# Interleaving the two halves of x and of the output weights in one tile, with a different run length in each block of a chunked-attention and gated-FFN kernel

## The chip, the cores and the metric

The kernel runs on one core of a Trainium2 chip. The metric is the device time of one execution in microseconds (us), lower is better. Each number of the trace comes from one execution recorded by the hardware profiler.

## The reference

Attention within chunks of 64 positions, then a gated feed-forward layer on the attention's output. Cut to what is computed:

```python
# q, k, v: (8, 8, 576, 64) float32; chunk = 64
scores = np.matmul(q_c, k_c.transpose(0, 1, 2, 4, 3)) / np.sqrt(64)
attn = np.exp(scores - scores.max(-1, keepdims=True))
attn = attn / (attn.sum(-1, keepdims=True) + 1e-09)
x = np.matmul(attn, v_c)          # laid out as 4608 tokens x 512
g, val = x @ w_gate, x @ w_val    # 512 x 1536 each
out = (g * sigmoid(g) * val) @ w_out      # 1536 x 512
```

## The kernel before

The 4608 tokens are cut into nine blocks (b = 0 to 8) of N = 512 tokens. In a block the attention writes x transposed: features on the 128 partitions in NK = 4 pieces k, the block's 512 tokens along the free axis. The feed-forward layer then goes through NF = 12 pieces f of 128 hidden features. For each f TensorE makes

- the gate (`gate`, g = 0) and the value (`value`, g = 1), each one PSUM bank of 128 x 512, and
- the projection (`project`), which multiplies the hidden piece by 128 rows of the output weights and adds into four PSUM banks `ps_o`, one for each 128 tokens, over all twelve f.

All these products are made in `float32r`, a 32-bit type of reduced precision, so each factor is split into an upper half (the rounded value) and a lower half (the remainder), and a product is the sum of three matmuls: lower times upper, upper times lower, upper times upper. The helper `split` (L62) makes the halves: ScalarE casts to the upper half (L64), VectorE subtracts it from the source to get the lower (L65).

A matmul has a stationary operand of 128 x 128, loaded by LDWEIGHTS, and a moving operand of 128 x 512 that is streamed past it. In the gate and the value (`some`, L419, matmul on L423) the stationary operand is a piece of the gate or value weights and the moving operand is x: `xh` or `xl`, 512 neighbouring words in each partition. In the projection (L466 to L469) the stationary operand is a 128-token piece of the hidden features (`hh` or `hl`) and the moving operand is the output weights of this f: `woh` or `wol`, again 512 neighbouring words.

So a block has 12 x 2 x 12 = 288 matmuls on L423 and 12 x 4 x 3 = 144 on L467 to L469, 432 in all, every one with 512 columns.

The halves of x are made once for a block: in blocks 0, 1 and 2 by `upper` (L541, ScalarE) and `lower` (L545, VectorE) from PSUM, in the later blocks by `ready` and `split` from the tile `s_sb`. They lie in the pool `xs`, tiles `xh0`, `xl0`, `xh1`, `xl1`, two buffers each. The halves of the output weights are made anew for each f of each block by `out_weights` (L425) from weights that stay in SBUF; they lie in the pool `wp`, tiles `woh` and `wol`, two buffers each. Two of these buffers also serve at the start as a place for attention values of block 1 (L526).

The order of the work on TensorE, ScalarE and VectorE is the order of the code (`manual_schedule`). Blocks 0 and 1 are interleaved while the weights are still being loaded and unpacked; the projections of block 1 are put off and follow together with the attention of block 2. Blocks 2 to 8 are written by `block` (L795): for each f the gate, the value, the output weights, and then, by `lag`, the projection of the f before; the attention of block b + 1 is spread between the f's of block b.

## Time and profile before

| quantity | value |
|---|---|
| time, median of two runs | 952.54 us (952.51 and 952.57) |
| the profiled execution's own time | 953.59 us |
| its span, first to last instruction | 951.8 us |
| TensorE's granted clock over the span | 1.0 |
| busy: PE, PEld, DVE, ACT | 944.4, 779.2, 479.5, 337.2 us |

PE is TensorE's matmul stream, PEld its loading of stationary operands, DVE is VectorE, ACT is ScalarE, POOL is GpSimd and SP the engine that issues most DMAs. The row of a group of instructions names the line of the code, the engine, the operation, the tile written and the tiles read, the shape, the number of instructions and after the bar their busy time and the mean duration of one in ns. Matmuls overlap each other in the pipeline, so the duration of one (390 ns for 512 columns) is longer than the distance from one to the next; what the stream takes is read from start times. A row of a table by stretches of time has the length of the stretch, then the busy time and the number of instructions of each engine.

### The profile page before, as it was taken

How to read it: one execution, taken by the hardware profiler on the slowest of the kernel's cores; microseconds unless marked ns; L12 is line 12 of the kernel's file. 1: busy time of each engine (PE TensorE's matmuls, PEld its weight loads, DVE VectorE, ACT ScalarE, POOL GpSimd, SP SyncE). 2: the span in 40 equal slices, each digit the busy share in tenths (PEclk: the TensorE clock that was granted, in tenths of full speed). 3: DMA queues.
4: the chain of work that ended last, by engine and by line, in shares of the span. 5: the costliest groups of instructions: out<-in, count | busy, mean ns of one | idle time of the engine just before them, and what ended most of it. 6: DMA issues, size and time to landing. Idle time of an engine off the chain costs nothing.

```text
span 951.8 us, 14613 instructions
## 1 busy us (share of the span) xinstructions
PE 944.4 (99%) x6299; PEld 779.2 (82%) x6299; DVE 479.5 (50%) x783; ACT 337.2 (35%) x540; POOL 6.6 (1%) x14
## 2 busy tenths in 40 slices
PE   8999999999999999999999999999999999999998
PEld 6788888888888888888888888888888888888886
DVE  6966666573465236632574347533663256432221
ACT  4745444265242333233323233233423342332222
POOL 1100000000000000000000000000000000000000
PEclk9999999999999999999999999999999999999999
DMA  9514322443300230021102030023002210000001
GB/s 360 216 68 155 155 108 103 156 166 112 89 1 1 90 87 3 1 90 63 27 0 88 2 90 1 3 86 90 1 1 89 67 23 1 1 15 30 1 1 44
DMA packets 43792, 63.85 MB, mean 67 GB/s; under 512 B 27472, under 2 KB 27472, under 8 KB 42320
## 3 DMA queue, kind: packets, MB, share of 16 engines
q1 hardware_dynamic: 42000, 59.78, 18.3%
q10 hardware_dynamic: 1728, 3.15, 0.9%
q8 instruction: 49, 0.80, 0.3%
q14 instruction: 15, 0.12, 0.0%
HBM read 50.33 MB, written 12.58 MB: 66 GB/s over the span
## 4 chain that ended last, share of the span: by engine, by line
PE 98%; DMA 1%; DVE 0%; SPq 0%; issue 0%; ACT 0%
PE ps_gv L423 62%; PE ps_o L467 10%; PE ps_o L468 10%; PE ps_o L469 10%; PE ps_a L226 2%; PE ps_a L306 1%; DMA qk_t<-in_qk 1%; PE ps_a L412 1%; PE ps_a L398 1%; PE ps_a L364 0%; DVE s_sb L392 0%; PE unread L60 0%; DVE top L358 0%; SPq L200 0%; ACT o_sb L474 0%
## 5 line engine op out<-in xcount | busy, mean ns | idle before, releaser
L423 PE MATMUL ps_gv<-xh,w 128*128 128x512 f32 x1728 | 531.1, 390 | 0.0
L423 PEld LDWEIGHTS ps_gv<-xh,w 128*128 128x128 f32 x1728 | 324.0, 188 | 67.2 <-issue 0.2
L423 PE MATMUL ps_gv<-xl,w 128*128 128x512 f32 x864 | 335.8, 391 | 0.0
L448 DVE SCALAR_TENSOR_TENSOR h<-ps_gv,h 128x512 f32<-128x512 f32 x108 | 74.6, 691 | 364.1 <-PE ps_gv L423 357.4
L423 PEld LDWEIGHTS ps_gv<-xl,w 128*128 128x128 f32 x864 | 162.2, 188 | 34.8 <-issue 0.4
L441 ACT ACTIVATE h<-ps_gv 128x512 f32<-128x512 f32 x108 | 64.6, 599 | 312.4 <-PE ps_gv L423 312.3
L467 PE MATMUL ps_o<-woh,hl 128*128 128x512 f32 x432 | 168.4, 390 | 0.0
L468 PE MATMUL ps_o<-wol,hh 128*128 128x512 f32 x432 | 168.1, 389 | 0.0
L469 PE MATMUL ps_o<-woh,hh 128*128 128x512 f32 x432 | 168.1, 389 | 0.0
L64 ACT CAST hh<-h 128x512 fp32r<-128x512 f32 x96 | 59.7, 621 | 183.3 <-DVE h L448 183.3
L467 PEld LDWEIGHTS ps_o<-woh,hl 128*128 128x128 f32 x432 | 81.1, 188 | 16.9
L469 PEld LDWEIGHTS ps_o<-woh,hh 128*128 128x128 f32 x432 | 81.1, 188 | 16.8
L468 PEld LDWEIGHTS ps_o<-wol,hh 128*128 128x128 f32 x432 | 81.1, 188 | 16.7
L293 DVE STREAM_TRANSPOSE turned<-s_sb 32x256 f32<-32x256 f32 x192 | 83.6, 436 | 2.7
L65 DVE TENSOR_TENSOR wol<-wo,woh 128x512 fp32r<-128x512 f32 x108 | 73.8, 684 | 13.1 <-ACT woh L64 13.0
L65 DVE TENSOR_TENSOR hl<-h,hh 128x512 fp32r<-128x512 f32 x96 | 66.4, 692 | 18.2 <-ACT hh L64 11.1
L64 ACT CAST woh<-wo 128x512 fp32r<-128x512 f32 x108 | 66.2, 613 | 15.6 <-DVE wo L102 15.6
L226 PEld LDWEIGHTS ps_a<-qk_t 64*64 64x64 f32 x1152 | 18.5, 137 | 5.0 <-issue 3.0
L226 PE MATMUL ps_a<-qk_t 64*64 64x64 f32 x1152 | 20.3, 223 | 0.5 <-DMA qk_t<-in_qk 0.4
L99 DVE TENSOR_TENSOR t<-t 128x1024 bf16<-128x1024 bf16 (+1 forms) x13 | 8.5, 651 | 22.7 <-ACT t L91 22.5
L474 ACT ACTIVATE o_sb<-ps_o 128x512 f32<-128x512 f32 x36 | 18.8, 599 | 2.2 <-PE ps_o L469 2.0
L136 ACT CAST w<-t 128x1024 fp32r<-128x1024 f32 x11 | 11.6, 1056 | 16.7 <-DVE t L102 16.7
(63 smaller groups left out, 411.5 us busy)
## 6 DMA issues: line engine op xcount, KB each, us to landing
raw<-in_wgv SPq DMA_DIRECT2D x11, 1024.0 KB, 7.0
qk_t<-in_qk SPq DMA_DIRECT2D x10, 1024.0 KB, 7.7
out<-o_sb SPq DMA_DIRECT2D x36, 256.0 KB, 2.3
qk_t<-in_qk SPq DMA_DIRECT2D x16, 512.0 KB, 4.0
raw<-in_wo SPq DMA_DIRECT2D x6, 1024.0 KB, 4.9
v_t<-in_v SPq DMA_DIRECT2D x28, 128.0 KB, 2.8
h<-h ACTq DMA_DIRECT2D x12, 256.0 KB, 2.0
h_in<-h SPq DMA_DIRECT2D x6, 512.0 KB, 3.6
```

The lines of the kernel that those rows point to most:

```text
L64: nc.scalar.copy(out=hi, in_=src)
L65: (engine or nc.vector).tensor_tensor(out=lo, in0=src, in1=hi.bitcast(F32), op=ALU.subtract)
L136: nc.scalar.copy(out=self.w[:, 0], in_=self.t)
L226: nc.tensor.matmul(ps[h][j * C:(j + 1) * C, i, u // 2, :], part[:, us:us + C], part[:, M * P + us:M * P + us + C], start=not more or i + u ...
L293: nc.vector.transpose(out=self.turned[to:to + 32, p:p + 2, j, :, 32 * (i % 2):32 * (i % 2) + 32], in_=src[32 * i:32 * i + 32, :, o // 2, 3 ...
L423: nc.tensor.matmul(ps, w, x, start=first and (k, i) == which[0], stop=last and (k, i) == which[-1])
L441: nc.scalar.activation(h, pg, AF.Silu, scale=2.0 ** -8)
L448: nc.vector.scalar_tensor_tensor(out=h, in0=pv, scalar=2.0 ** -8, in1=h, op0=ALU.mult, op1=ALU.mult)
L467: nc.tensor.matmul(o, hl[:, ts], woh, start=f == 0, stop=False)
L468: nc.tensor.matmul(o, hh[:, ts], wol, start=False, stop=False)
L469: nc.tensor.matmul(o, hh[:, ts], woh, start=False, stop=f == NF - 1)
L474: nc.scalar.activation(o_sb, o, AF.Copy, scale=2.0 ** -8)
```

## The change

The upper and the lower half no longer have tiles of their own. They share a tile twice as wide and lie in it in alternating runs of g columns: g words of the upper half, g words of the lower, and so on. The run length depends on the block: `RUN` gives 512 (N), 512, 1, 2, 16, 32, 64, 128 and 256 for blocks 0 to 8. With 512 the two halves lie one behind the other, as two tiles would. In the blocks with a shorter run the 512 words of a half are spread over 1024 words: with g = 1 every second word is taken, with g = 2 two words of every four, with g = 256 two stretches of 256 words.

```diff
+RUN = (N, N, 1, 2, 16, 32, 64, 128, 256)
 class Attn:
         def places(self):
-            self.x = [(xs.tile([P, 2, N], F32R, name=f"xh{c}"), xs.tile([P, 2, N], F32R, name=f"xl{c}"))
-                      for c in range(NP // 2)]
+            self.x = []
+            for c in range(NP // 2):
+                x = xs.tile([P, 2 * 2 * N], F32R, name=f"x{c}").rearrange(
+                    "p (i n o g) -> p i n o g", i=2, o=2, g=RUN[self.b])
+                self.x.append((x[:, :, :, 0], x[:, :, :, 1]))
...
+    def runs(a, g):
+        return a.rearrange("p (n g) -> p n g", g=g)
...
     def some(ps, a, f, g, which, first=True, last=True):
...
-            nc.tensor.matmul(ps, w, x, start=first and (k, i) == which[0], stop=last and (k, i) == which[-1])
+            nc.tensor.matmul(runs(ps, RUN[a.b]), w, x, start=first and (k, i) == which[0], stop=last and (k, i) == which[-1])
 
-    def out_weights(f, engine=None):
-        woh = wp.tile([P, DM], F32R, name="woh")
-        wol = wp.tile([P, DM], F32R, name="wol")
-        split(wo_raw[f], woh, wol, engine)
+    def out_weights(f, b, engine=None):
+        w = wp.tile([P, 2 * DM], F32R, name="wo").rearrange("p (n o g) -> p n o g", o=2, g=RUN[b])
+        woh, wol = w[:, :, 0], w[:, :, 1]
+        split(runs(wo_raw[f], RUN[b]), woh, wol, engine)
         return woh, wol
...
-            ts, o = slice(t * P, (t + 1) * P), a.o[t]
+            ts, o = slice(t * P, (t + 1) * P), runs(a.o[t], RUN[a.b])
...
-            pool, tag = (ld, "v_t") if a is a0 else (wp, ("woh", "wol")[c])
+            pool, tag = (ld, "v_t") if a is a0 else (wp, "wo")
```

`upper`, `lower` and `ready` view their source through `runs` in the same way, so that source and target have the same shape. In the built program the PSUM output of every matmul is still 512 neighbouring words, the stationary operands are as before, and the number and the order of the instructions on PE, ACT, DVE, POOL and SP are the same as before. What differs is the pattern in which three kinds of operand are laid out in SBUF: the moving operand of the 432 matmuls of each of the blocks 2 to 8, the targets of the ScalarE casts and of the VectorE subtractions that make the halves, and the subtraction's second input.

On VectorE, in block 3 (the ninth and the tenth f), the rows before are, with `wol` and `xl` the lower halves written and `xh` and `woh` the upper halves read:

```order
L448 SCALAR_TENSOR_TENSOR h<-ps_gv,h 128x512
L65 TENSOR_TENSOR wol<-wo_1357,woh 128x512
L65 TENSOR_TENSOR hl<-h,hh 128x512
L448 SCALAR_TENSOR_TENSOR h<-ps_gv,h 128x512
L65 TENSOR_TENSOR wol<-wo_1457,woh 128x512
L65 TENSOR_TENSOR hl<-h,hh 128x512
L65 TENSOR_TENSOR xl_3829<-s_sb,xh_3828 128x512 x2
```

And the same place after the change, where `x` and `wo` hold both halves:

```order
L457 SCALAR_TENSOR_TENSOR h<-ps_gv,h 128x512
L67 TENSOR_TENSOR wo<-wo_1346,wo 128x256x2
L67 TENSOR_TENSOR hl<-h,hh 128x512
L457 SCALAR_TENSOR_TENSOR h<-ps_gv,h 128x512
L67 TENSOR_TENSOR wo<-wo_1445,wo 128x256x2
L67 TENSOR_TENSOR hl<-h,hh 128x512
L67 TENSOR_TENSOR x_3774<-s_sb,x_3774 128x32x16 x2
```

No instruction has moved. The output weights of block 3 are written as 256 runs of 2 words; the x written here is already that of block 4, in 32 runs of 16.

More of the change, by code (lines that the diff above doesn't have):

```diff
@@ L322, in ready @@
             for p in range(p, p + n):
-                split(self.s[:, p].rearrange("p c h k -> p (c h k)"), *(x[:, p % 2] for x in self.x[p // 2]))
+                split(runs(self.s[:, p].rearrange("p c h k -> p (c h k)"), RUN[self.b]),
+                      *(x[:, p % 2] for x in self.x[p // 2]))
     class First(Attn):
@@ L473, in project @@
                 o_sb = pool.tile([P, DM], F32, name="o_sb", tag=tag)
-                nc.scalar.activation(o_sb, o, AF.Copy, scale=2.0 ** -8)
+                nc.scalar.activation(o_sb, a.o[t], AF.Copy, scale=2.0 ** -8)
                 r = a.b * N + t * P
@@ L540, in upper @@
     def upper(a, px, p):
-        nc.scalar.copy(out=x_of(a, p)[0], in_=px[p % 2])
+        nc.scalar.copy(out=x_of(a, p)[0], in_=runs(px[p % 2].rearrange("p u k -> p (u k)"), RUN[a.b]))
     def lower(a, px, p):
         hi, lo = x_of(a, p)
-        nc.vector.tensor_tensor(out=lo, in0=px[p % 2], in1=hi.bitcast(F32), op=ALU.subtract)
+        nc.vector.tensor_tensor(out=lo, in0=runs(px[p % 2].rearrange("p u k -> p (u k)"), RUN[a.b]), in1=hi.bitcast(F32),
+                                op=ALU.subtract)
     o_banks, a_banks = (ps_o, "ps_o"), (ps_a, "ps_a")
@@ L669, in attn_then_gated_ffn @@
     p0 = parts(a0, 0, h0)
-    wo_f = out_weights(0)
+    wo_f = out_weights(0, 0)
     lag(p0, wo_f)
@@ L701, in attn_then_gated_ffn @@
         down[f + 1].scale()
-        wo_f = out_weights(f)
+        wo_f = out_weights(f, 0)
         lag(p0, wo_f)
@@ L715, in prepare @@
         p = parts(a1, f, late[-1][:, f % 2])
-        return p, out_weights(f)
+        return p, out_weights(f, 1)
     f, o = NF - 1, down[NF - 1]
@@ L732, in attn_then_gated_ffn @@
     p0 = parts(a0, f, h0)
-    wo_f = out_weights(f)
+    wo_f = out_weights(f, 0)
     lag(p0, wo_f)
@@ L824, in between @@
                 middle.get(f, lambda: None)()
-                wo_f.extend(out_weights(f))
+                wo_f.extend(out_weights(f, b))
             h = gated(a, f)
```

## The prediction

> **What bounds the kernel now.** I read the page's first two parts and the chain of work that ended last, then the groups by line with shapes kept apart, then the chain in order of time, then the stretches of time by block.

> ```profile
> PE 944.4 (99%) x6299; PEld 779.2 (82%) x6299; DVE 479.5 (50%) x783; ACT 337.2 (35%) x540; POOL 6.6 (1%) x14
> PEclk9999999999999999999999999999999999999999
> PE 98%; DMA 1%; DVE 0%; SPq 0%; issue 0%; ACT 0%
> PE ps_gv L423 62%; PE ps_o L467 10%; PE ps_o L468 10%; PE ps_o L469 10%; PE ps_a L226 2%; PE ps_a L306 1%; DMA qk_t<-in_qk 1%; PE ps_a L412 1%; PE ps_a L398 1%; PE ps_a L364 0%; DVE s_sb L392 0%; PE unread L60 0%; DVE top L358 0%; SPq L200 0%; ACT o_sb L474 0%
> ```

> TensorE's matmul stream is the bound: 99% busy, 98% of the chain that ends last, at full granted clock in every slice. 92% of the chain (62 + 3 x 10) are the matmuls on L423 and L467 to L469, whose moving operands the change re-lays.

> ```profile
> L423 PE MATMUL ps_gv<-xh,w 128*128 128x512 f32 x1728 | 531.1, 390 | 0.0
> L423 PE MATMUL ps_gv<-xl,w 128*128 128x512 f32 x864 | 335.8, 391 | 0.0
> L468 PE MATMUL ps_o<-wol,hh 128*128 128x512 f32 x432 | 168.1, 389 | 0.0
> ```

> The idle time before them is 0.0: they follow each other without a gap. Whatever one of them takes longer is added to the span at once. How far apart they are is seen in the chain in order of time, where 24 matmuls of one f (gate and value) are one row:

> ```profile
> 496.99 5.44 PE ps_gv L423 x24
> 505.15 5.44 PE ps_gv L423 x24
> ```

> From one f to the next are 505.15 - 496.99 = 8.16 us for 24 + 12 matmuls, so **226.7 ns per matmul**, or 0.443 ns per column, whether it reads x or output weights. The stretches of blocks 2 and 3 (length first, then busy time and count of PE, PEld, DVE, ACT):

> ```profile
> 232.30:335.00 102.70, 102.68 (x690) 85.01 (x690) 50.77 (x85) 32.31 (x53) 0.00 (x0) 1.00 0.15 46
> 335.00:438.00 103.00, 103.00 (x692) 85.33 (x691) 50.23 (x84) 32.31 (x53) 0.00 (x0) 1.00 0.13 42
> ```

> A block takes about 102.8 us, of which 432 x 0.2267 = 97.9 are the matmuls in question; VectorE has 52 us free in it, ScalarE 70.

> **The change part by part.** No instruction is added, removed or moved; what can change is how long an instruction takes whose operand is now spread.

> *The matmuls with runs of 1 (block 2).* No row shows TensorE reading a moving operand with a step. The nearest rows are ScalarE reads of every second 32-bit word (L84 and L91 read one half of 64-bit inputs), beside casts of neighbouring words:

> ```profile
> L84 ACT ACTIVATE t<-raw 128x1024 f32<-128x1024 f32 x11 | 12.6, 1142 | 0.0
> L84 ACT ACTIVATE wo<-raw 128x512 f32<-128x512 f32 x12 | 8.1, 674 | 2.5 <-DMA raw<-in_wo 2.5
> L91 ACT ACTIVATE t<-raw 128x1024 bf16<-128x1024 uint32 x11 | 12.1, 1103 | 0.0
> L91 ACT ACTIVATE o_sb<-raw 128x512 bf16<-128x512 uint32 x12 | 7.9, 659 | 0.0
> L136 ACT CAST w<-t 128x1024 fp32r<-128x1024 f32 x11 | 11.6, 1056 | 16.7 <-DVE t L102 16.7
> L161 ACT CAST w<-t 128x512 fp32r<-128x512 f32 x2 | 1.2, 622 | 0.0
> ```

> The difference between 1024 and 512 words is free of fixed cost: (1142 - 674)/512 = 0.914 ns and (1103 - 659)/512 = 0.867 ns per word at a step of 8 bytes, against (1056 - 622)/512 = 0.848 with neighbours. So at ScalarE's pace a step of 8 bytes costs 2 to 8%, and the read passes over 8 bytes in 0.867 ns: 9.2 bytes per ns. TensorE's present stream passes over 4 bytes in 0.443 ns: 9.0 bytes per ns. No row of the trace shows a read that passes over more. With runs of 1, TensorE at its present pace would have to pass over 18 bytes per ns. If about 9 is what one reader gets, a matmul that spans 4096 bytes in place of 2048 takes 512 x 0.867 = 444 ns by L91, 468 by L84, 453 as twice its present time. The other end is no cost, if TensorE's reader can do what no row asks of it. I take 444 ns, by the cheaper of the two nearest rows: +217 ns a matmul, and 432 x 0.2173 = **+93.9 us**. A gain is excluded: the same columns are streamed at a clock already at its full value.

> *Runs of 2 (block 3).* Again 4096 bytes are spanned, by 8 wanted and 8 skipped. Between no cost and +217 ns, the gap of 8 bytes is nearer to the 4-byte gap of L84 and L91 than to the long gaps of the next rows, so I take the full price: **+93.9 us**.

> *Runs of 16 to 256 (blocks 4 to 8).* They span 4096 bytes too, but the skipped bytes are whole stretches of 64 to 1024 bytes. The nearest rows write (L378) and read (L384) runs of 64 words with 64 skipped, beside neighbouring words (L441, L243):

> ```profile
> L378 ACT ACTIVATE s_sb<-ps_a 128x512 f32<-128x512 f32 x8 | 4.8, 596 | 5.1 <-PE ps_a L364 5.1
> L441 ACT ACTIVATE h<-ps_gv 128x512 f32<-128x512 f32 x108 | 64.6, 599 | 312.4 <-PE ps_gv L423 312.3
> L384 DVE TENSOR_REDUCE z<-s_sb 128x8 f32<-128x512 f32 x12 | 7.6, 678 | 0.0
> L243 DVE TENSOR_REDUCE top<-ps_a 128x8 f32<-128x512 f32 x12 | 8.2, 682 | 0.0
> ```

> 596 against 599 and 678 against 682: a long gap between long runs costs nothing. Gaps of 64 bytes and more are nearer to these 256 than to 4, so I take **0** for 5 x 432 matmuls; the other end is 93.9 us for each block.

> *The casts and subtractions.* A block has 12 + 4 of each with spread targets:

> ```profile
> L64 ACT CAST woh<-wo 128x512 fp32r<-128x512 f32 x108 | 66.2, 613 | 15.6 <-DVE wo L102 15.6
> L65 DVE TENSOR_TENSOR wol<-wo,woh 128x512 fp32r<-128x512 f32 x108 | 73.8, 684 | 13.1 <-ACT woh L64 13.0
> DVE h L448 <- PE ps_gv L423: 357.4, 87, 8.4
> 503.15 0.68 DVE L65 TENSOR_TENSOR wol<-wo,woh 128x512 fp32r<-128x512 f32 x1
> 503.92 0.69 DVE L65 TENSOR_TENSOR hl<-h,hh 128x512 fp32r<-128x512 f32 x1
> 510.43 0.39 PE L467 MATMUL ps_o<-woh,hl 128*128 128x512 f32 x1
> ```

> No row has a spread write of single words. Doubling bounds it: 16 x 0.684 = 10.9 us on VectorE and 16 x 0.613 = 9.8 on ScalarE per block, into 52 and 70 us free. In one f, the halves end at 503.92 + 0.69 = 504.61 and are first read at 510.43, so 5.8 us cover some 2.6 of delay (two doubled operations). If that cover went, the projection would start late. VectorE's wait for value matmuls (357.4 us in all) says what has the slack. The tightest place is the start of block 2, where VectorE writes the last lower halves of x just ahead of TensorE:

> ```profile
> 231.54 1.28 DVE L545 TENSOR_TENSOR xl<-ps_a,xh 128x512 fp32r<-128x512 f32 x2
> 233.83 0.40 PE L423 MATMUL ps_gv<-xl,w 128*128 128x512 f32 x1
> ```

> The pair is ready at 232.8 and its first half is needed at 233.83, the third k. Doubled, the first half would be ready at 232.9 and the second at 234.1, still ahead. I take **0**; at most 1 us.

> *The shared tile.* Freeing `woh` and `wol` together delays nothing, since their last readers are two neighbouring matmuls (226.7 ns). At the start `out_weights(0)` takes a buffer that GpSimd filled with values:

> ```profile
> 24.01 2.69 POOL L349 COPY v_t<-v_t 64x512 f32<-64x512 f32 x4 [8.06 <-DMA v_t<-in_v]
> 42.98 0.62 ACT L64 CAST woh<-wo 128x512 fp32r<-128x512 f32 x1 [0.27 <-DVE wo L102]
> ```

> The copies end at 26.7, 16 us before the cast, and their readers on TensorE stand ahead of the matmuls that the cast's step waits for: **0**.

> *Sum.* 951.8 + 2 x 93.9 = 1139.6 us of span. The profiled execution took 953.59 us, 1.05 above the median of 952.54, so against the median it is 952.5 + 187.8 = 1140.3: **1140 us**.

> **The rivals.**

> *Not slower: TensorE's reader has room.* The price is 0 and the time 952 us, within 2% (what a measurement of this kernel can tell from no change). It decides where 8 bytes of span take 0.443 ns or less for TensorE, half of what ScalarE shows. For it speaks that ScalarE never asked for more than 9.4 bytes per ns (8/0.848), so its rows bound its reader from one side only; against it, that L84 and L91 are already 2 to 8% late at that pace, as if at the edge. I give it 0.15. [...]

> *Only runs of 1 are slow.* If a reader fetches aligned pieces of 8 bytes, one per 0.867 ns for ScalarE and one per 0.886 (two columns) for TensorE, a run of 2 is one piece and runs of 1 waste half of each. Both row groups fit this as well as wider pieces. The time is 952.5 + 93.9 = 1046 us. I give it 0.15; the byte span argues against it but cannot exclude it. [...]

> *Steeper.* Runs of 1 could be read one word per fetch, or runs of 16 cost as well. One further block at +93.9 us gives 1234 us, and more is possible. Against it are ScalarE's 2 to 8% and L378's 596 ns. I give it 0.05.

> **How the numbers follow.** Both short runs at about double: 0.65, 1140 us, with its own range of 1136 to 1161 (twice 226.7 ns gives 952.5 + 864 x 0.2267 = 1148; L84's 468 ns gives 952.5 + 864 x 0.2413 = 1161; and 1136 if a few ns per matmul are fixed and do not double). Only runs of 1: 0.15. No cost: 0.15. Steeper: 0.05. The range that holds 8 in 10 takes the first two: from 1035, a little under 1046 for a price somewhat below double, to 1165. Slower by over 2% are the first two and the steeper one, 0.85; within 2% 0.14 and faster 0.01 share the case without a cost.

> **What would show it right or wrong.** In the profile after, the start times of 24 matmuls of one f tell each step. Right: about 440 to 455 ns apart in blocks 2 and 3, 227 from block 4 on, with the whole difference in two stretches of about 197 us. ScalarE and VectorE casts at 613 to 700 ns with no new wait of TensorE on them. If block 3 stays at 227 ns, the 8-byte piece is right; if both do, TensorE's reader has room; if block 4 is slow, the free gap fell. Idle time ahead of TensorE with 227 ns between matmuls would mean that the spread writes, which I cost at nothing, decide instead.

## The result and the profile after

The changed kernel takes 1157.45 us (1157.42 and 1157.48) against 952.54: a ratio of 1.2151, interval 1.2099 to 1.2203. The profiled span is 1155.7 us, and the granted clock was 1.0. The forecast of 1140 us, with a range of 1035 to 1165, has the direction and nearly the size.

The page of the changed kernel, first the busy times, then the slices of PEld, the chain by engine and two groups of matmuls:

```profile
PE 1148.5 (99%) x6299; PEld 795.9 (69%) x6299; DVE 479.6 (41%) x783; ACT 339.1 (29%) x540; POOL 6.1 (1%) x14
PEld 6888888844444444444445777777788888888887
PE 98%; DMA 1%; DVE 0%; SPq 0%; issue 0%; ACT 0%
L432 PE MATMUL ps_gv<-x,w 128*128 128x512 f32 x2592 | 743.3, 447 | 0.0
L477 PE MATMUL ps_o<-wo,hh 128*128 128x512 f32 x432 | 192.8, 446 | 0.0
```

TensorE is still the whole chain and still idles 0.0 ahead of its matmuls; no other engine has taken over. PE's busy time rose by 1148.5 - 944.4 = 204.1 us, and the time by 204.9. The slices of PEld show where: as many weight loads, but spread thin (4 in place of 8) in thirteen slices of 28.9 us, and a little thin (5, 7) in the eight behind them. Before, the same row was

```profile
PEld 6788888888888888888888888888888888888886
```

The chain in order of time (start in us, duration in us, then engine, tile, line and count) has 24 gate and value matmuls of one f as one row, so that the duration divided by 24 is the time of one. Neighbouring f's of blocks 2, 3, 4 and 5, and one of block 6:

```profile
280.29 10.88 PE ps_gv L432 x24
296.61 10.88 PE ps_gv L432 x24
...
480.07 10.83 PE ps_gv L432 x24
496.31 10.83 PE ps_gv L432 x24
...
659.23 5.79 PE ps_gv L432 x24
667.88 5.78 PE ps_gv L432 x24
...
767.21 5.70 PE ps_gv L432 x24
775.76 5.70 PE ps_gv L432 x24
...
873.26 5.44 PE ps_gv L432 x24
```

From one f to the next are 24 + 12 matmuls. Block 2 (runs of 1): 16.32/36 = 453.3 ns each; block 3 (runs of 2): 16.24/36 = 451.1; block 4 (runs of 16): 8.65/36 = 240.3; block 5 (runs of 32): 8.55/36 = 237.5; from block 6 on (runs of 64 and more) 5.44/24 = 226.7, as before. The sum is 432 x (226.6 + 224.4 + 13.6 + 10.8) ns = 205.4 us, against 204.9 measured. Nothing is left to explain outside the matmuls' own pace.

The casts that write spread words did become slower. These are the casts made during block 2 (shortest, median and longest in ns): `wo` goes into runs of 1 and takes 28 ns more than the mean of 613 before; `x` is already that of block 3, goes into runs of 2 and takes 42 more than 620:

```profile
L66 ACT CAST wo<-wo x10: 636/641/642, 270.0 to 418.9; 128x512 fp32r<-128x512 f32 x10
L66 ACT CAST x<-s_sb x4: 657/662/668, 392.6 to 409.4; 128x512 fp32r<-128x512 f32 x4
```

No wait of TensorE on them appeared. VectorE's subtractions into spread words took 682 to 686 ns in the median, before 681 (`wol`) and 685 (`xl`).

### The profile page after: what moved, and what is told of

It is laid out like the page before. It is cut to its first block, busy times and chain, and to the rows that moved or that the text cites. A ratio compares the mean times of both kernels' runs of the same rounds, so it can differ in the third digit from the quotient of the medians.

```text
span 1155.7 us, 14595 instructions
## 1 busy us (share of the span) xinstructions
PE 1148.5 (99%) x6299; PEld 795.9 (69%) x6299; DVE 479.6 (41%) x783; ACT 339.1 (29%) x540; POOL 6.1 (1%) x14
## 4 chain that ended last, share of the span: by engine, by line
PE 98%; DMA 1%; DVE 0%; SPq 0%; issue 0%; ACT 0%
PE ps_gv L432 63%; PE ps_o L476 10%; PE ps_o L477 10%; PE ps_o L478 10%; PE ps_a L228 2%; PE ps_a L308 1%; DMA qk_t<-in_qk 1%; PE ps_a L418 1%; PE ps_a L404 0%; PE ps_a L370 0%; PE unread L62 0%; DVE top L364 0%; DVE s_sb L398 0%; SPq L202 0%; ACT o_sb L483 0%
## 5 line engine op out<-in xcount | busy, mean ns | idle before, releaser
L432 PE MATMUL ps_gv<-x,w 128*128 128x512 f32 x2592 | 743.3, 447 | 0.0
L432 PEld LDWEIGHTS ps_gv<-x,w 128*128 128x128 f32 x2592 | 496.6, 192 | 225.0 <-issue 138.7
L476 PE MATMUL ps_o<-wo,hl 128*128 128x512 f32 x432 | 192.9, 447 | 0.0
L477 PE MATMUL ps_o<-wo,hh 128*128 128x512 f32 x432 | 192.8, 446 | 0.0
L478 PE MATMUL ps_o<-wo,hh 128*128 128x512 f32 x432 | 192.4, 445 | 0.0
L450 ACT ACTIVATE h<-ps_gv 128x512 f32<-128x512 f32 x108 | 64.6, 598 | 421.1 <-PE ps_gv L432 421.0
L476 PEld LDWEIGHTS ps_o<-wo,hl 128*128 128x128 f32 x432 | 83.1, 192 | 37.8 <-issue 23.4
L478 PEld LDWEIGHTS ps_o<-wo,hh 128*128 128x128 f32 x432 | 83.0, 192 | 37.7 <-issue 23.4
L477 PEld LDWEIGHTS ps_o<-wo,hh 128*128 128x128 f32 x432 | 83.0, 192 | 37.6 <-issue 23.5
L67 DVE TENSOR_TENSOR wo<-wo,wo 128x512 fp32r<-128x512 f32 x108 | 73.8, 684 | 10.5 <-ACT wo L66 10.4
L66 ACT CAST wo<-wo 128x512 fp32r<-128x512 f32 x108 | 66.8, 619 | 15.4 <-DVE wo L104 15.4
L311 ACT COPY s_sb<-ps_a 128x512 f32<-128x512 f32 x24 | 12.3, 599 | 20.0 <-PE ps_a L308 20.0
L138 ACT CAST w<-t 128x1024 fp32r<-128x1024 f32 x11 | 11.6, 1055 | 16.7 <-DVE t L104 16.7
```

The lines of the kernel that those rows point to most:

```text
L66: nc.scalar.copy(out=hi, in_=src)
L67: (engine or nc.vector).tensor_tensor(out=lo, in0=src, in1=hi.bitcast(F32), op=ALU.subtract)
L311: nc.scalar.copy(out=self.s[:, p:p + n, :, j], in_=px[j])
L432: nc.tensor.matmul(runs(ps, RUN[a.b]), w, x, start=first and (k, i) == which[0], stop=last and (k, i) == which[-1])
L450: nc.scalar.activation(h, pg, AF.Silu, scale=2.0 ** -8)
L476: nc.tensor.matmul(o, hl[:, ts], woh, start=f == 0, stop=False)
```

## The experiments

All kernels compute the same; they differ in where the words of an operand lie (of x and of the output weights, in e7 of the hidden features), and in the order in which the columns are written and read. Words are 4 bytes. A *piece* is 16 aligned bytes, four words. Places are counted from the start of the tile; that the tiles themselves start on a 16-byte edge (in e9 on a 256-byte one) is an assumption, as no view tells where a tile lies. A *four* is four successive columns of a matmul, counted from its first. *Full rate* is about 227 ns for the 512 columns of a matmul, *half rate* about 453. Unless it is said otherwise, each of the blocks 2 to 8 has a pattern of its own, so that one kernel tries seven, and the pace of a block is read from its own rows; a time without an interval is that of one execution. The granted clock was 1.0 or 0.999 in all of them. The first column of the tables of rows is the start in us, the second the duration of 24 gate and value matmuls. Edits are shown against the changed kernel (in e12 against the kernel before), and `...` stands for lines left out.

The first theory is the prediction's: a reader gets about 9 bytes per ns of the span it passes over, skipped bytes included, and runs long enough escape in some way. Its rivals: that the share of each fetched piece that is used decides; that the spread writes, not the reads, cost the time.

### e1: the run lengths in between

```diff
-RUN = (N, N, 1, 2, 16, 32, 64, 128, 256)
+RUN = (N, N, 4, 8, 32, 16, 64, 2, 4)
```

> Run lengths 4, 8, 32, 16, 64, 2, 4 in blocks 2 to 8, for x and for the output weights. Theory of pieces: TensorE reads a moving operand in aligned pieces of 16 bytes, one per about 1.77 ns (226.7 ns for the 128 pieces of a dense row), so runs of 4 and 8 words waste nothing: 227 to 241 ns per matmul in every block but block 7 (runs of 2), which takes 451 ns; time 1060 to 1080 us. Theory of the span (the prediction's): what counts is the bytes passed over as long as the gap is short, so runs of 4 and 8 cost as much as runs of 2, about 451 ns in blocks 2, 3, 7 and 8; time about 1350 us. Theory of runs: every start of a run costs the same 0.88 ns (224 ns for 256 runs), so runs of 4 take 339 ns and runs of 8 take 283; time about 1180 us. The small extra of runs of 16 and 32 (14 and 11 ns) follows the pattern into the swapped blocks 5 and 4 if it is the pattern's, and stays at blocks 4 and 5 if it belongs to the place.

Measured: 1068.78 us, with 953.33 for the kernel before on the same chip. One f of blocks 2 (runs of 4), 3 (of 8) and 7 (of 2), from the chain in order of time:

```profile
276.33 5.57 PE ps_gv L432 x24
...
381.17 5.60 PE ps_gv L432 x24
...
840.95 10.88 PE ps_gv L432 x24
```

Runs of 4 take 5.57/24 = 232 ns, runs of 8 take 233, and runs of 2 in another block 453 again. So the step is between 2 and 4. With runs of 4 the read passes over 4096 bytes in 232 ns, 17.7 bytes per ns. The span theory falls here: the skipped bytes cost next to nothing (232 against 226.7 ns) where whole pieces are skipped. Nor does each start of a run have one price, by which runs of 4 would have taken 339 ns and runs of 8 283. Runs of 32 and 16, now in blocks 4 and 5, take 237.5 and 241 ns: their small extra went along with the pattern and did not stay with the block.

### e2: x or the output weights alone

```diff
+RUN = (N, N, 1, N, 2, N, 16, N, 32)
+OUT_RUN = (N, N, N, 1, N, 2, N, 16, N)
...
-        w = wp.tile([P, 2 * DM], F32R, name="wo").rearrange("p (n o g) -> p n o g", o=2, g=RUN[b])
+        w = wp.tile([P, 2 * DM], F32R, name="wo").rearrange("p (n o g) -> p n o g", o=2, g=OUT_RUN[b])
...
```

> x alone in runs of 1, 2, 16, 32 in blocks 2, 4, 6, 8; the output weights alone in runs of 1, 2, 16 in blocks 3, 5, 7. If the price is that of the moving read, only the matmuls that read the spread operand are slow: the gate and value matmuls at 453 and 451 ns in blocks 2 and 4 with the projections at 227, the projections at 453 and 451 in blocks 3 and 5 with gate and value at 227; time 952.5 + 288 x (0.2264 + 0.2244) + 144 x (0.2264 + 0.2244) + about 9 for the runs of 16 and 32 = 1156 us. If instead the spread writes of ScalarE and VectorE slow TensorE (through memory that they share, or by late halves), all matmuls of a block slow down together, or idle time stands ahead of TensorE.

Measured: 1158.99 us (before: 953.33). Two neighbouring f's of block 2 (x in runs of 1) and of block 3 (output weights in runs of 1):

```profile
302.18 10.87 PE ps_gv L433 x24
315.80 10.87 PE ps_gv L433 x24
...
453.65 5.46 PE ps_gv L433 x24
464.55 5.46 PE ps_gv L433 x24
```

In block 2 the matmuls that read x take 453 ns, and the 12 of the projection the remaining 13.62 - 10.87 = 2.75 us, 229 each. In block 3 it is the other way: 5.46/24 = 227.5, and (10.90 - 5.46)/12 = 453. Each kind of matmul pays by its own moving operand, and both by the same price. If the spread writes were the cause, all matmuls of a block would be slow.

### e3: four-way interleaving, a shift and a permutation

```diff
+LAY = ("2", N), ("2", N), ("4", 1), ("4", 2), ("4", 4), ("+2", 4), ("0213", 0), ("4", 16), ("4", 8)
...
+                x = xs.tile([P, 2 * 2 * N + 4], F32R, name=f"x{c}")
+                x = x[:, 2:2 + 4 * N] if how == "+2" else x[:, :4 * N]
+                if how == "0213":
+                    x = x.rearrange("p (i o n b a) -> p i o n a b", i=2, o=2, a=2, b=2)
...
+                elif how == "4":
+                    x = x.rearrange("p (n i o g) -> p i o n g", i=2, o=2, g=g)
...
```

Only x is re-laid. "4" puts four halves in one tile, "+2" starts runs of 4 in the middle of a piece, "0213" reads the four words of each piece in that order.

> Only x is spread, the output weights are dense. In the tile of 2048 words lie four halves (two feature pieces, each upper and lower). Blocks 2, 3, 4: one run of all four after the other with runs of 1, 2, 4 words (16, 8 and 16 wanted bytes in strides of 16, 32 and 64 bytes: one word in each 16 bytes; two words in every second 16 bytes; all of every fourth). Block 5: runs of 4, two-way, but the tile starts 8 bytes into a 16-byte piece, so that each run lies across two pieces. Block 6: dense halves, but read in the word order 0, 2, 1, 3 within each 16 bytes. Blocks 7 and 8: four-way runs of 16 and 8. Theory of pieces, 1.77 ns each: 512 pieces and 907 ns in block 2, 256 and 451 to 453 in blocks 3 and 5, 227 to 241 in blocks 4, 6, 7 and 8; time 1280 to 1295 us. Theory of the span: 907 ns in blocks 2, 3, 4 and 8, 453 in block 5, 227 in block 6; about 1800 us. Theory of neighbours (what counts is whether the next word read is the next in memory, not where the piece begins): block 5 as fast as runs of 4 on the boundary, block 6 at 451 or more.

Measured: 1170.41 us (before: 953.33). Blocks 2 (one word of each piece), 4 (runs of 4, three pieces skipped), 5 (runs of 4 across two pieces) and 6 (the order 0, 2, 1, 3):

```profile
307.38 11.05 PE ps_gv L444 x24
...
620.44 5.57 PE ps_gv L444 x24
...
751.37 10.87 PE ps_gv L444 x24
...
892.81 5.52 PE ps_gv L444 x24
```

One word of each piece takes 11.05/24 = 460 ns, hardly more than two of each: so it isn't "one piece per 1.77 ns", by which it would have taken twice as long. Two words of every second piece (block 3) take 462. Three skipped pieces are as free as one (232). But four neighbouring words that lie across two pieces take 453. The order inside a piece does next to nothing (230). All this fits a first theory of fours: a four goes at full rate if its words lie in one piece, otherwise at half rate, however many pieces they touch.

### e4 and e5: the spread writes alone, and long runs alone

```diff
+RUN = (N,) * NB
...
+        if b > 1:
+            w = t.rearrange("p (n o g) -> p n o g", o=2, g=1)
+            split(runs(wo_raw[f], 1), w[:, :, 0], w[:, :, 1], engine)
...
```

e4 keeps all halves in neighbouring words, and in blocks 2 to 8 makes the output weights' halves twice: first into every second word, then again into the place where they are read. e5 has the run lengths 64, 64, 128, 128, 256, 256, 64 in blocks 2 to 8.

> All blocks dense (run length 512) for what TensorE reads, in the shared tile. In blocks 2 to 8 the halves of the output weights are written twice: first word by word alternating (as with runs of 1), then dense over it, so ScalarE has 84 more casts and VectorE 84 more subtractions, at about 0.64 and 0.68 us. If the writes and the shared tile are hidden, as the prediction has it, the time is that of the kernel before, 952.5 us within 0.5. If they decide, it is longer by up to 84 x 0.68 = 57 us.

> Run lengths 64, 64, 128, 128, 256, 256, 64 in blocks 2 to 8, for x and the output weights. If a gap between runs of 64 words and more is free for TensorE, as blocks 6 to 8 of the changed kernel show (226.7 ns per matmul), the time is 952.5 us within 1. If any interleaving has a price, as runs of 32 had (11 ns per matmul), it would be up to 3024 x 0.011 = 33 us more.

Measured: e4 954.03 us, ratio 1.0009 (1.0000 to 1.0018), e5 953.10 us, ratio 0.9998 (0.9989 to 1.0007), both against 953.05. In e4 the groups of casts and subtractions of the output weights (count, busy us and mean ns, idle time before) read

```profile
L67 DVE TENSOR_TENSOR wo<-wo,wo 128x512 fp32r<-128x512 f32 x192 | 132.0, 688 | 69.9 <-ACT wo L66 69.8
L66 ACT CAST wo<-wo 128x512 fp32r<-128x512 f32 x192 | 120.7, 629 | 260.0 <-DVE wo L67 244.7 <-DVE wo L104 15.3
```

Against 73.8 and 66.2 us before, VectorE works 58 us and ScalarE 55 us more, and the time grows by at most 0.2%. The writes of the output weights are hidden even when they are made twice. In e5 3024 matmuls read runs of 64 to 256, and the time is that of the kernel before (953.10 against 953.05 us); in the changed kernel the matmuls with runs of 64, 128 and 256 keep 226.7 ns. Runs of 64 and more are free here.

### e6, e7 and e9: where neighbouring words lie

e3 left open whether a four whose words lie across two pieces is slow in neighbouring words too. e6 starts x, in neighbouring words, 1, 2, 3 and 4 words later (blocks 2 to 5), moves its second half by two words (block 6), and starts runs of 8 in the middle of a piece (block 7); its tiles of x are 64 bytes longer.

```diff
+LAY = ("d", 0), ("d", 0), ("d", 1), ("d", 2), ("d", 3), ("d", 4), ("h", 256), ("+2", 8), ("d", 0)
...
+                x = xs.tile([P, 4 * N + 16], F32R, name=f"x{c}")
+                if how == "d":
+                    x = x[:, g:g + 4 * N].rearrange("p (i o n) -> p i o n", i=2, o=2)
...
```

> Only x is laid out anew. Blocks 2 to 5: dense halves of 512 words that start 1, 2, 3 and 4 words after a 16-byte boundary. Block 6: the first 256 words of a half on the boundary, the other 256 at 2 words past one. Block 7: two-way runs of 8 that start 2 words past a boundary. Block 8: dense and on the boundary. Theory of fours: four columns that follow each other, counted from the matmul's first, are read at full rate only if all four lie in one aligned 16-byte piece, and otherwise at half rate, however many pieces they touch: 453 ns in blocks 2, 3, 4 and 7, 227 in blocks 5 and 8, 340 in block 6; time about 953 + 288 x 0.2264 x 4.5 = 1246 us. Theory of visits: what counts is how often the read comes to a new 16-byte piece, so a dense half costs 129 visits in place of 128 wherever it starts: 227 ns in blocks 2 to 6 and 8, about 340 in block 7 (three visits in eight words); time about 986 us.

Measured: 996.44 us (before: 953.11). Blocks 2 and 7:

```profile
278.94 5.69 PE ps_gv L440 x24
...
812.38 7.92 PE ps_gv L440 x24
```

Neighbouring words one word off the edge take 237 ns, two words off 234, three 230: nearly free, though each four then touches two pieces. The theory of fours, which had 453 here, falls. Only one of the two pieces is new, however: the other was read for the four before. Runs of 8 from the middle of a piece take 7.92/24 = 330 ns, about half way between full and half rate. In these the fours read 2 words of a first piece and 2 of a second (both new), then 2 of the second (which the four before read too) and 2 of a third. That suggests that the new pieces of a four count, and that fours with two take double. Block 8, laid out as in the kernel before but in the longer tiles, takes 230 instead of 226.7.

e7 asks for the stationary operand: `hh` and `hl` in every second word in blocks 2 to 4, in neighbouring words in block 5, two words further on in blocks 6 to 8; x and the output weights as before.

```diff
+RUN = (N,) * NB
+STEP = (1, 1, 2, 2, 2, 1, 1, 1, 1)
+AT = (0, 0, 0, 0, 0, 0, 2, 2, 2)
...
+        t = hp.tile([P, 2 * N + 4], F32R, name="hhl")[:, AT[a.b]:AT[a.b] + 2 * N]
+        t = t.rearrange("p (n o) -> p o n", o=2) if STEP[a.b] == 2 else t.rearrange("p (o n) -> p o n", o=2)
...
```

> All moving operands are dense and on the boundary. The stationary operand of the projections (the halves of the hidden features) is spread instead: alternating words in blocks 2 to 4, dense in block 5, dense but 2 words past a 16-byte boundary in blocks 6 to 8. If only the stream of the moving operand has the rule, all matmuls stay at 227 ns and the time at 953 us. If the loading of weights has it too, a load's 188 ns grow by 53 to 107 ns (128 columns at half rate) in blocks 2 to 4 and 6 to 8; at 241 to 295 ns a load no longer hides behind a matmul of 227, so the 144 projections of each of these six blocks take 14 to 70 ns longer: 965 to 1013 us.

Measured: 965.83 us (before: 953.11). That is the lower edge of what was expected if the loads had the rule, but by coincidence: all blocks are slower, by 2 to 3 ns a matmul (229 to 230) in the gate and value matmuls, which don't read these operands, and by 3 to 7 in the projections, block 5 with its unchanged layout too. These are blocks 2 and 5:

```profile
278.11 5.51 PE ps_gv L434 x24
...
589.89 5.49 PE ps_gv L434 x24
```

The loads of the projections (L479 to L481) take 190 ns in the mean of all nine blocks, those of the gate and the value 188. If the 2 ns belong to the three blocks with spread words alone, a load there is some 6 ns longer (an estimate: 2 x 9/3). That stays hidden: the projections take 231 to 233 ns in the blocks 2 to 4 and 230 to 234 in the others. What changed for every block is that the tile of the hidden features is 16 bytes longer, so tiles behind it may lie elsewhere. Whether a place alone can cost that much is what e9 asks: x in neighbouring words, starting 0, 16, 32, 64, 128, 192 and 256 bytes into the tile in blocks 2 to 8; the tile is 33 x 256 bytes long.

```diff
+LAY = ("d", 0), ("d", 0), ("d", 0), ("d", 4), ("d", 8), ("d", 16), ("d", 32), ("d", 48), ("d", 64)
...
+                x = xs.tile([P, 4 * N + 64], F32R, name=f"x{c}")
...
```

> All operands are dense; the halves of x begin 0, 16, 32, 64, 128, 192 and 256 bytes past a 256-byte boundary in blocks 2 to 8. Theory of placement: the small extra of 4 to 16 ns that runs of 4 to 32 and some dense rows show comes from where an operand lies with respect to 256 bytes (runs of 64 words fill such stretches, shorter ones do not), so blocks 2 and 8 stay at 226.7 ns and blocks 3 to 7 take 229 to 240; time 956 to 972 us. Theory of hops: the extra comes from the starts of runs, so a dense row has none wherever it begins: 226.7 ns in all blocks and 953 us.

Measured: 962.64 us (before: 953.38). Blocks 2, 4 and 8 (0, 32 and 256 bytes):

```profile
275.47 5.44 PE ps_gv L441 x24
...
483.04 5.60 PE ps_gv L441 x24
...
897.33 5.44 PE ps_gv L441 x24
```

226.7 ns at 0 and at 256 bytes, 229.6 to 233.3 at the others. A start 16 to 192 bytes into the tile costs 1 to 3% here. The extra of e7's gate and value matmuls is of that size; that it comes from shifted tiles is not shown, as no view tells where the tiles of e7 lie.

### e8: pieces read in part

```diff
+LAY = ("d", 0), ("d", 0), (1, 4), (1, 8), (3, 4), (2, 16), ("odd", 0), (2, 32), (0, 4)
...
+                elif how == "odd":
+                    x = x[:, :4 * N].rearrange("p (i o n b a) -> p i o n a b", i=2, o=2, a=2, b=4)
+                else:
+                    x = x[:, how:how + 4 * N].rearrange("p (i n o g) -> p i o n g", i=2, o=2, g=g)
...
```

Pairs are (first word, run length); "odd" reads the words 0, 2, 4, 6, then 1, 3, 5, 7 of each eight.

> Only x is laid out anew; all tiles begin on a 16-byte boundary and the runs at an offset. A visit is a stretch of columns that follow each other and lie in one aligned 16-byte piece. Block 2: two-way runs of 4 from word 1 (visits of 3 and 1 words); block 3: runs of 8 from word 1 (3, 4, 1); block 4: runs of 4 from word 3 (1, 3); block 5: runs of 16 from word 2 (2, 4, 4, 4, 2); block 6: dense halves, read in the order 0, 2, 4, 6, 1, 3, 5, 7 within each 32 bytes (visits of 2, no byte left out); block 7: runs of 32 from word 2; block 8: runs of 4 on the boundary. Theory of two: a visit costs 0.885 ns for its first word and as much for all further words together: 340, 283, 340, 283, 453, 255, 227 to 233 ns; time about 1126 us. Theory of full pieces: only a visit of all four words runs at 0.443 ns per word, any smaller one at 0.885 ns per word: 453, 340, 453, 283, 453, 255, 227 to 233 ns; time about 1207 us. In both, block 6 is at 453 ns though no byte is skipped; were it the skipped bytes that cost, it would be at 227.

Measured: 1179.54 us (before: 953.38). Blocks 5 (runs of 16 from word 2), 6 (odd) and 7 (runs of 32 from word 2):

```profile
754.68 6.79 PE ps_gv L441 x24
...
880.54 8.16 PE ps_gv L441 x24
...
1006.35 6.27 PE ps_gv L441 x24
```

283 ns is what one four in 4 at half rate makes, 261 nearly what one in 8 does: 1.25 and 1.15 times 226.7 (one in 8 alone would make 1.125, 255 ns; the other 6 ns are not explained). The even and odd words of each eight take 340, 1.5 times, as if of the two fours on the same two pieces only the first were slow. Both theories on record had 453 there and fall; that of two also had 340 for blocks 2 and 4, which took 454 and 463. Block 3 took 328. Nothing is skipped in block 6 and each byte is read once, so neither the skipped bytes nor the used share of the pieces decides; the pieces that a four needs anew fit.

### e10: how long a piece is held

```diff
+LAY = ("d", 0), ("d", 0), (2, 4), (2, 8), (2, 16), (4, 2), (4, 4), (2, 64), (8, 4)
...
+                    x = x.rearrange("p i o (n b a) -> p i o n a b", a=how, b=g)
...
```

Neighbouring words again, read in other orders: (2, 8) reads the even words of each 16, then the odd ones; (4, 2) reads 0, 4, 1, 5, 2, 6, 3, 7; (4, 4) reads 0, 4, 8, 12, 1, 5 and so on.

> Only the word order within dense halves of x is changed; every half fills its 512 words, tiles as in the kernel before. Block 2: even then odd words of each 32 bytes (0, 2, 4, 6, 1, 3, 5, 7). Block 3: even then odd words of each 64 bytes; block 4: of each 128 bytes; block 7: of each 512 bytes. Block 5: 0, 4, 1, 5, 2, 6, 3, 7 in each 32 bytes. Block 6: 0, 4, 8, 12, 1, 5, 9, 13 and so on in each 64 bytes. Block 8: 0, 8, 16, 24, 1, 9, 17, 25 and so on in each 128 bytes. Theory of new pieces: four columns in turn run at full rate if they need at most one aligned 16-byte piece that is not still held from the columns just before, and at half rate otherwise. Then blocks 2 and 5 take 340 ns (two pieces held suffice); block 3 takes 340 and blocks 6 and 8 take 283 if four pieces are held, and 453 to 460 if fewer are; block 4 takes 340 only if eight are held and block 7 only if 32 are, else 453. Theory of visits (a stretch of columns in one piece is slow unless it takes all four words; nothing is held): 453 to 460 ns in all seven blocks. Theory of skipped bytes: 227 ns in all seven.

Measured: 1212.24 us (before: 952.66). Blocks 3 (2, 8), 5 (4, 2) and 6 (4, 4):

```profile
440.96 11.53 PE ps_gv L435 x24
...
753.00 5.18 PE ps_gv L435 x24
...
859.02 6.44 PE ps_gv L435 x24
```

Blocks 2, 4, 7 and 8 took 340, 453, 453 and 269 ns. Block 5 had been expected at 340, and it decided: its first four reads words 0, 4, 1, 5, two new pieces, and yet it goes at 5.18/24 = 215.8 ns, faster than words in their own order. So "at most one new piece per four" falls as well. What tells 0, 4, 1, 5 from 0, 2, 4, 6 is which columns share a piece. In the first the two even columns of the four (words 0 and 1) lie in one piece and the two odd ones (words 4 and 5) in another; in the second each pair lies across both. From this came the last theory:

### e11: a test of the theory on new patterns

```diff
+DENSE = "(i o n b a)", 4, 1
+LAY = (DENSE, DENSE, ("(i n b a o)", 2, 2), ("(i n b o a)", 2, 2), ("(i o n b a)", 8, 2), ("(i o b n a)", 1, 2),
+       ("(i o b n a)", 2, 2), ("(i n b a o)", 4, 2), ("(n b a i o)", 2, 2))
...
+                x = x.rearrange(f"p {how} -> p i o {read}", i=2, o=2, a=n, b=m)
...
```

> Only x is re-laid or re-ordered, one pattern per block; the output weights stay in neighbouring words. The theory formed from the runs so far, and now tested on patterns it has not seen: columns are taken in fours; the two even ones and the two odd ones of a four are fetched apart; a four goes at full rate if neither pair needs more than one new aligned 16-byte piece, else at half. A rival: only the words of a four decide (how many pieces they lie in, and whether all words of a piece are used), not their order. Words read by four successive columns, the theory's ns per gate or value matmul, the rival's. Block 2: runs of 1, columns in the order 0, 2, 1, 3 (words 0, 4, 2, 6): 227 to 233, the rival 453. Block 3: runs of 2, the same order (words 0, 4, 1, 5): 227 to 233, the rival 451. Block 4: neighbouring words in the order 0, 8, 1, 9: 216 to 227, the rival 216 to 227 too. Block 5: 0, 256, 1, 257: 216 to 227, the rival 453. Block 6: 0, 1, 256, 257: half of the fours at half rate, 340; the rival as block 5. Block 7: runs of 1, words 0, 8, 2, 10, 4, 12, 6, 14: 216 to 233, the rival 453. Block 8: one word of each piece, words 0, 8, 4, 12: 460 by both. Time by the theory: 952.5 + 288 x 0.113 + 288 x 0.233 - 2 x 288 x 0.011 = 1046 us if blocks 4 and 5 take 216, 1052 with 227.

Measured: 1039.65 us (before: 952.82). One f of each of the blocks 2 to 8:

```profile
241.42 5.52 PE ps_gv L437 x24
...
344.79 5.52 PE ps_gv L437 x24
...
447.86 5.18 PE ps_gv L437 x24
...
547.53 5.18 PE ps_gv L437 x24
...
649.97 8.15 PE ps_gv L437 x24
...
781.95 5.24 PE ps_gv L437 x24
...
887.34 10.36 PE ps_gv L437 x24
```

Divided by 24: 230, 230, 215.8, 215.8, 340, 218 and 432 ns. In blocks 2 and 3 x takes the same words at the same gaps as in the blocks 2 and 3 of the change, and only the order of the columns within each four differs: 230 in place of 453 and 451. Block 5 alternates between words 1024 bytes apart and takes 215.8; block 6, with the same distance but the pairs crossed, takes 340. The rival, by which the words of a four decide and not their order, falls. One size was wrong: block 8 was expected at 460 and took 432, just twice 215.8.

### e12: a version that beats both

```diff
...
+    def mixed(a):
+        return a.rearrange("p (n a b) -> p n b a", a=4, b=2)
+    def near(a):
+        return a.rearrange("p (n b a) -> p n b a", a=4, b=2)
+    def order(a):
+        return a.rearrange("p (n b a) -> p n a b", a=4, b=2)
+    def natural(a):
+        return a.rearrange("p (n a b) -> p n a b", a=4, b=2)
...
-            nc.tensor.matmul(ps, w, x, start=first and (k, i) == which[0], stop=last and (k, i) == which[-1])
+            nc.tensor.matmul(natural(ps), w, order(x), start=first and (k, i) == which[0], stop=last and (k, i) == which[-1])
...
-        split(wo_raw[f], woh, wol, engine)
-        return woh, wol
+        w = wp.tile([P, 2, DM], F32R, name="wo")
+        split(mixed(wo_raw[f]), near(w[:, 0]), near(w[:, 1]), engine)
+        return order(w[:, 0]), order(w[:, 1])
...
```

In e10 the casts that wrote x in this order, one word of a piece at a time, took 1160 ns (shortest, median and longest of two), against 662 in the change:

```profile
L66 ACT CAST x<-s_sb x2: 1160/1160/1160, 696.1 to 697.1; 128x512 fp32r<-128x512 f32 x2
```

So here the casts and subtractions write neighbouring words, and their source is read with a step of two.

> A version meant to beat both kernels: x and the output weights are stored so that the columns, taken in their order, read the words 0, 4, 1, 5, 2, 6, 3, 7 of each eight, in all nine blocks; the casts and subtractions write neighbouring words and read their source with a step of two words. Theory: the order alone sets the pace, 215.8 ns a matmul as in block 5 of the run before, for x and for the output weights: 9 x 432 x 0.0109 = 42 us less, 910 us. If only the x matmuls gain (2592 of 3888): 924 us. Rivals: in blocks 0 and 1 loading and unpacking, not TensorE, set the pace, so that the gain there is lost: 7 x 4.7 = 33 us less, 920 us. The casts and subtractions with a stepped source take longer and TensorE waits for them: idle time in front of it, 940 us or more. Nothing gained outside of one block: 952 us.

Measured: 910.82 us (910.40 to 911.21), ratio to the kernel before 0.9556, interval 0.9541 to 0.9572. The page's group of the gate and value matmuls (count, busy us and mean ns, idle time before):

```profile
L438 PE MATMUL ps_gv<-x,w 128*128 128x512 f32 x2592 | 577.7, 380 | 0.2
```

The casts of the output weights, in the groups with shapes kept apart:

```profile
L64 ACT CAST wo<-wo 128x512 fp32r<-128x512 f32 x108 | 71.4, 661 | 14.8 <-DVE wo L102 14.8
```

Two neighbouring f's of block 2 in the chain in order of time:

```profile
257.11 5.18 PE ps_gv L438 x24
264.88 5.18 PE ps_gv L438 x24
```

5.18/24 = 215.8 ns for x and (7.77 - 5.18)/12 = 215.8 for the output weights. Over nine blocks that is 3888 x 10.9 ns = 42.4 us, and 952.82 - 910.82 = 42.0 were gained. The casts are 48 ns longer (661 against 613) and TensorE doesn't wait for them: 0.2 us idle ahead of the 2592 matmuls.

## Why the prediction was right, and where its reasons were not

**The bound.** Right. With TensorE idle 0.0 before and after, each ns of a matmul's pace went into the time: 205.4 us from the spacing, 204.9 measured.

**Runs of 1.** The price was right to 4%: +226.6 ns in place of +217, 97.9 us in place of 93.9. The reason was wrong. The 444 ns were taken from the bytes per ns that ScalarE passes over; e1 has TensorE pass over 17.7 bytes per ns at runs of 4. By the theory that e11 bore out, each pair of a four needs two new pieces there, so that every four goes at half rate: twice 226.7 = 453.4, a value that stood in the prediction beside the 444. That the two nearly agree is luck.

**Runs of 2.** Right again (+224.4 ns against +217), and again by luck: the choice went by how near the 8-byte gap is to the rows' gaps, and the distance of a gap does not decide. e11 reads words 1024 bytes apart at 215.8 ns (block 5).

**Runs of 16 to 256.** Here a term was mis-sized. Blocks 6 to 8 cost 0, as taken and as e5 shows. Blocks 4 and 5 cost 13.6 and 10.8 ns a matmul, 432 x 24.4 ns = 10.5 us in place of 0. Rows of ScalarE and VectorE with runs of 64 were asked about runs of 16 and 32; runs of 64 are free for TensorE as well, shorter ones not quite, and e1 and e2 find the same extra for the same run lengths in other blocks. e9 has small extras even without a gap, by the start in the tile (up to 233.3 ns), but doesn't derive 240; why runs of 16 cost more than runs of 4 (240 against 232) stays open.

**The difference to the forecast.** 432 x (9.3 + 7.1) ns = 7.1 us from the two short runs and 10.5 from blocks 4 and 5 make 17.6; the difference between 1157.45 and 1140 is 17.5.

**Casts, subtractions, the shared tile.** Right: 28 to 42 ns more for a ScalarE cast, at most 2 for VectorE, no new wait; e4 shows it with the writes made twice. (Two doubled operations would have meant about 1.3 us of delay in one f, not 2.6; nothing hung on it.)

**A gain.** The prediction held it to be excluded, as the clock was full. That reason was wrong: e12 streams the same columns in 215.8 ns in place of 226.7 at the same granted clock, 1.0. The change itself has no block with such an order, so the forecast didn't suffer.

**The rivals.** "Not slower" fell in blocks 2 and 3: 453 and 451 ns against 226.7. In another order of the columns the same words take 230 ns (e11). "Only runs of 1 are slow" fell with block 3: runs of two neighbouring words on an 8-byte edge take those 451 ns. "Steeper" did not come in either form: runs of 1 take no more than twice 226.7 ns, and runs of 16 cost 6%, not a further 93.9 us; even one word of each piece (e3) takes only 460.

**What is inferred.** The two separate fetches of a four fit all the patterns here and foretold e11's, but no row shows a fetch; another mechanism with the same consequences isn't excluded. Its sizes are not exact either: patterns of the same class lie between 215.8 and 243 ns at full rate and between 432 and 480 at half, and mixed patterns miss the sum of the two by up to 15 ns (283 against 268 in e10, block 6).

## What to carry to other kernels

The rule was tried with matmuls of 128 x 128 by 128 x 512 in `float32r` alone. When such a moving operand doesn't lie in neighbouring words, write down the words that four successive columns read: where columns 0 and 2, and columns 1 and 3, each lay in one aligned 16-byte piece, a matmul took 216 to 243 ns here; where a pair of every four went to two new pieces, it took 432 to 480, and this kernel, bound by TensorE, paid all of it (205.4 us by the spacing, 204.9 in the time). Gaps between whole pieces were free or cost up to 7% (226.7 to 242.9 ns), and the order of the columns is as much a means as the layout is. A price read from another engine's row may come out right by chance: one experiment at the next size (here runs of 4) tells whether its reason holds.

## What the runs showed that was not expected

- Neighbouring words in their own order are not the fastest: the order 0, 4, 1, 5, 2, 6, 3, 7 takes 215.8 ns per 512 columns against 226.7 (e10, e12), and so do 0, 8, 1, 9 and 0, 256, 1, 257 (e11). This gave 4.4% on a kernel that was bound by these matmuls. Each pair then stays in one piece for two fours. Whether this is the reason is open: e11's block 7, where each pair goes to a new piece with every four (words 0, 2, then 4, 6), takes 218 ns, while its blocks 2 and 3, which also do, take 230.
- The start of a moving operand in its tile changes the pace: 226.7 ns at 0 and 256 bytes, as much as 233.3 between (e9).
- Reading the even, then the odd words of each 16 takes 480 ns (e10, block 3), more than twice 226.7 or 215.8; half rate is not quite the floor.
- ScalarE writes runs of 1 and 2 words in 636 to 668 ns (the changed kernel), but words that alternate between two pieces in 1160 (e10).
- A stationary operand in every second word in three of nine blocks makes the mean load only 2 ns longer (190 against 188, e7), where a moving operand in every second word doubles the matmul (453 against 226.7, the changed kernel).
